# A linear-attention and mixture-of-experts kernel: four unread products at the start, and one PSUM bank in two halves for block 0's query work

## The chip, the cores and the metric

The kernel runs on one core of a Trainium2 chip. The metric is the device time of one execution, in microseconds (us). The core has a matrix engine (TensorE, PE in the profile; PEld is its weight load), VectorE (DVE), ScalarE (ACT), GpSimd (POOL) and SyncE (SP), which here only issues DMAs.

## The reference

Three parts follow each other; only the first matters for the change. Keys and queries are projected by the same weight, every row is shifted by its largest magnitude, and exp of plus and minus the result gives 256 features. The key features are summed against the values over each batch's 576 positions, and the query features are multiplied by that sum and divided by the denominator.

```
proj = einsum('bhsd,df->bhsf', x, w_phi)          # x is q or k; 64 -> 128
proj = proj - max(abs(proj), axis=-1)
phi  = concatenate([exp(proj), exp(-proj)], -1)
kv = einsum('bhsf,bhsd->bhfd', k_p, v);  z = sum(k_p, axis=2)
out = einsum('bhsf,bhfd->bhsd', q_p, kv) / (einsum('bhsf,bhf->bhs', q_p, z) + 1e-6)
```

There are 4 batches of 8 heads; the 2304 rows of all batches stand in a row. Behind it come an RMS norm with a gated layer (512 to 1536 to 512) and a soft mixture of 8 experts, both over all 2304 rows.

## The kernel before

The kernel has a first stage (keys, values, and the first block of queries), a long middle that runs over six blocks of 384 rows, and the experts' products at the end. All three are one program, whose order on each engine a scheduler lays out from dependencies and buffers.

**Tiles.** The first stage takes 18 tiles `ks[i]` of 128 rows. For each one `Front.project` (L503) makes two PSUM banks `P` with 8 products of 128 columns, four from weight rows 0 to 63 and four from rows 64 to 127, alternating. VectorE takes the largest magnitude (`mx`, L507) and the difference (`pr`, L511), ScalarE two exponentials (`kp`, L524 and L525). Then `kv_of` (L548) multiplies the features by the values `vt`: 4 products of 256 columns into `kacc0` and 4 into `kacc1`, with outputs that alternate between partitions 0 to 63 and 64 to 127. `z_of` (L557) makes 8 sums of 32 output partitions into `kacc2`. The loop projects tile i+2 while it multiplies tile i. After a batch's last row, `Evac` copies the three sums out, and `Evac.turn` (L585) transposes them through a bank `kvt`, which ScalarE or VectorE copies to `kv` (L594, L596).

**Block 0's queries.** `Rows`, a kind of `Turned`, handles the first 384 query rows. For each of four pairs of heads, c = 0 to 3, it makes three products `P` of 256 columns from `qraw` (`project`, L389; VectorE reads them as `qmx` and `qpr`), turns each with two transposes `T` (`turn`, L404; ScalarE reads them with two exponentials `e`, L406), and then multiplies with `kv` (`attend`, tile `o`, L449). `TURNED0` says into which half step of the key loop each one falls.

**PSUM.** There are eight banks. Three hold `kacc0` to `kacc2`; two have the tag `P` and hold the key projections; three have the tag `misc`, in turn for the first tile's two key projections, for `kvt`, for the queries' `P` and `T`, for `o` and for the last transposes `yT`. A buffer of `misc` can be written when the last reader of what it held has ended.

**The start.** `WARM = 3` products `idle` (L609) of a zeroed tile `still` run before anything has landed; nobody reads them. SyncE issues the loads of the first key tiles, values, constants and `qraw`. Between the tiles stands the conversion of nine weight pieces (`Conv`: `wraw`, 1 MB each, two ScalarE and three VectorE passes and a cast).

Of the kernel before, what the change touches and what calls it, by code (L numbers as in the profile page):

```python
# [7 lines left out]
F32 = mybir.dt.float32  # L8
# [8 lines left out]
NB, NH, SEQ, HD, DF = 4, 8, 576, 64, 128  # L17
# [3 lines left out]
TILES = NT // 128  # L21
# [7 lines left out]
KCONV, MCONV = (3, 2), (2, 2)  # L29
NX = 4  # L30
CFIRST = 7
WARM = 3
NLEFT = 2
ELEFT = 4
CTURN = 4
# [32 lines left out]
def tile_kernel(ctx: ExitStack, tc: tile.TileContext, q2T, qT, kT, v, wbd, wg, wv, wo, rmsg, phi, w1, w2, consts, out):  # L68
# [19 lines left out]
    def pool(stack, name, space=None, bufs=1, side="left"):  # L88
        kw = {} if space is None else {"space": space}
        if space is None:  # L90
            kw["side"] = side
        if space is not DRAM:
            kw["reuse_waits"] = "tile"
        return stack.enter_context(tc.tile_pool(name=name, bufs=bufs, **kw))
# [37 lines left out]
    class Conv:  # L132
# [3 lines left out]
        def __init__(self, sp, wp, key, bufs):  # L136
            self.sp, self.wp, self.key, self.bufs, self.n = sp, wp, key, bufs, 0
# [54 lines left out]
    kvt = {}  # L192
# [12 lines left out]
    class Q:  # L205
# [3 lines left out]
        def __init__(self, sp, ps, blk, bufs):  # L209
            self.sp, self.ps, self.blk, self.bufs = sp, ps, blk, bufs  # L210
            self.raw, self.x, self.e = {}, {}, {}

        def psum(self, name, shape):
            return self.ps.tile(shape, F32, tag="misc", name=name, bufs=self.bufs["misc"])

        def numerator(self, c, e):
            if c == 0:
                xraw[self.blk] = xp.tile([128, 4, BLK], F32, tag="xraw", name="xraw", bufs=1)
            num = self.psum("num", [128, BLK])
            for b, t0, t1 in block_parts(self.blk):  # L220
                for s in range(2):
                    for hh in range(2):
                        PE.matmul(out=num[64 * hh:64 * hh + 64, t0:t1], lhsT=kvt[b][:, 2 * c + hh, s, 0:HD],  # L223
                                  rhs=e[hh][:, s, t0:t1], start=s == 0, stop=s == 1, skip_group_check=True)
            return num
# [152 lines left out]
    class Turned(Q):  # L378
# [5 lines left out]
                SP.dma_start(out=self.raw[c], in_=q2T[self.blk, c])  # L384

        def project(self, c, i):
            p = self.psum("P", [128, 2, DF])
            o = p.rearrange("p h f -> p (h f)")
            PE.matmul(out=o, lhsT=self.raw[c][:, 128 * i:128 * i + 128], rhs=wbd_f, start=True, stop=True)  # L389
            mx = self.sp.tile([128, 2, 1], F32, tag="mx", name="qmx", bufs=2)  # L390
            self.pr = self.sp.tile([128, 2, DF], F32, tag="pr", name="qpr", bufs=self.bufs["pr"])
            DVE.tensor_reduce(out=mx, in_=p, axis=AX.X, op=ALU.max, apply_absolute_value=True)
            DVE.tensor_tensor(out=self.pr, in0=p, in1=mx.to_broadcast([128, 2, DF]), op=ALU.subtract)
            if i == TPB - 1:
                self.load(c + self.bufs["raw"])
            return self.pr

        def turn(self, c, i, pr):
            if i == 0:
                self.e2 = self.sp.tile([128, 2, 2, BLK], F32, tag="e", name="e2", bufs=self.bufs["e"])  # L400
                self.e[2 * c], self.e[2 * c + 1] = self.e2[:, 0], self.e2[:, 1]
            tp = self.psum("T", [128, 2, 128])
            for h in range(2):
                PE.transpose(out=tp[:, h], in_=pr[:, h], identity=ident)  # L404
            for s in range(2):
                ACT.activation(out=self.e2[:, :, s, 128 * i:128 * i + 128], in_=tp, func=AF.Exp, scale=1.0 - 2.0 * s)  # L406
# [72 lines left out]
    with ExitStack() as pk:  # L479
        kx = pool(pk, "kx")  # L480
        sp = pool(pk, "spk")
        psk = pool(pk, "psk", PSUM)
# [78 lines left out]
        class Evac:  # L561
# [17 lines left out]

            def turn(self, n):  # L580
                kv = self.kv
                tp = psk.tile([128, 2, 2, 128], F32, tag="misc", name="kvt", bufs=3)
                for c in range(2):
                    for s in range(2):
                        PE.transpose(out=tp[:, c, s], in_=self.sb[n][:, c, s], identity=ident)  # L585
                for c in range(2):
                    if n < 2:
                        o = kv[:, 4 * c + n:4 * c + n + 3:2, :, 0:HD].rearrange("p h s d -> p s h d")
                        i = tp[:, c].rearrange("p s (h d) -> p s h d", h=2)
                    else:  # L590
                        o = kv[:, c::2, :, HD].rearrange("p h s -> p s h")
                        i = tp[:, c].rearrange("p s (h r) -> p s h r", h=4)[:, :, :, 0]
                    if n == 1:
                        DVE.tensor_copy(o, i)  # L594
                    else:
                        ACT.copy(out=o, in_=i)  # L596
                if n == 2 and self.b >= 2:
                    SP.dma_start(out=kv_d[self.b], in_=kv.rearrange("p h s d -> p (h s d)"))

        kb = {"tag": "k", "raw": 4, "pr": 3, "P": ("P", 2)}  # L600
        ks = [K(sp, psk, kT, i, kb if i else dict(kb, P=("misc", 3))) for i in range(TILES)]
        ks[0].load(ACT)
        SP.dma_start(out=wbd_f, in_=wbd)
        still = sp.tile([128, 256], F32, tag="kvs0", name="still", bufs=1)
# [2 lines left out]
        idle = psk.tile([32, 256], F32, tag="acc0", name="idle", bufs=1)  # L607
        for _ in range(WARM):
            PE.matmul(out=idle, lhsT=still[:, 0:32], rhs=still, start=True, stop=True)  # L609
# [15 lines left out]
                k.shift(hf)  # L625
                k.exps(hf)
        fillers = []
        q0 = Rows(sp, psk, 0, {"misc": 3, "raw": 2, "pr": 3, "e": 2})
        qsteps = q0.steps(TURNED0[0:4], TURNED0[4:8], TURNED0[8:])
        qsteps = [[f for m, f in qsteps if m == n] for n in range(2 * TILES)]  # L630
        q0.begin()
# [87 lines left out]
    with ExitStack() as p2:  # L719
# [5 lines left out]
        sp = pool(tctx, "conv")  # L725
# [4 lines left out]
        def post(blk, x2):  # L730
# [177 lines left out]
            if blk == NBLK - 1:  # L908
                return finish
            return [turn(o) for o in range(TPB)] + [logits, rows, dturn, dispatch, combine, cturn]  # L910


# [19 lines left out]
        def gate(m, xs):  # L932
            g = wide("g", m, xs)
            t = mp.tile([128, BLK], F32, tag="t", name="t", bufs=2)
            ACT.activation(out=t, in_=g, func=AF.Tanh, scale=0.5)  # L935
            DVE.scalar_tensor_tensor(out=t, in0=t, scalar=1.0, in1=g, op0=ALU.add, op1=ALU.mult)  # L936
            return t
# [21 lines left out]
        t = gate(0, xs)  # L959
# [8 lines left out]
        for blk in range(NBLK):  # L968
            acc = [ps.tile([128, DM], F32, tag=f"acc{i}", name=f"acc{i}", bufs=1) for i in range(TPB)]
            qsteps, qnext = qnext or [], None  # L970
            if blk == 1:
                q1ctx.close()
                sp = pool(pctx, "post", side="right")
            if blk == NBLK - 1:
# [5 lines left out]
                sp = pool(pctx, "post", side="right")  # L980
# [32 lines left out]
            for m in range(MF):  # L1013
# [3 lines left out]
                if more:  # L1017
                    t = gate((m + 1) % MF, xs)
# [34 lines left out]
    with ExitStack() as p3:  # L1053
        sp = pool(p3, "sp3")
# [145 lines left out]
```

## Time and profile before

| what | us |
|---|---|
| runs of the kernel, lowest, median, highest | 705.16, 706.3, 707.02 |
| profiled execution | 705.7 |
| its span, first to last instruction | 703.9 |
| TensorE busy in the span | 689.4 (98%) |
| VectorE, ScalarE, GpSimd busy | 468.5, 329.1, 147.2 |
| first stage, to the first product of the middle | about 118 |

A busy share of 98% says that TensorE is rarely without an instruction. It does not say that each instruction goes as fast as it could: two products that use different rows or different output partitions of the array can run at once, and both count as busy. So the stage is read by the start times of its groups of products, and by the wait that each row shows in brackets.

### The profile page before, as it was taken

How to read it: one execution, taken by the hardware profiler on the slowest of the kernel's cores; microseconds unless marked ns; L12 is line 12 of the kernel's file. 1: busy time of each engine (PE TensorE's matmuls, PEld its weight loads, DVE VectorE, ACT ScalarE, POOL GpSimd, SP SyncE). 2: the span in 40 equal slices, each digit the busy share in tenths (PEclk: the TensorE clock that was granted, in tenths of full speed). 3: DMA queues.
4: the chain of work that ended last, by engine and by line, in shares of the span. 5: the costliest groups of instructions: out<-in, count | busy, mean ns of one | idle time of the engine just before them, and what ended most of it. 6: DMA issues, size and time to landing. Idle time of an engine off the chain costs nothing.

```text
span 703.9 us, 11807 instructions
## 1 busy us (share of the span) xinstructions
PE 689.4 (98%) x4653; PEld 571.3 (81%) x4653; DVE 468.5 (67%) x915; ACT 329.1 (47%) x687; POOL 147.2 (21%) x74
## 2 busy tenths in 40 slices
PE   7999999999999999999999999999999999999995
PEld 4667766988889898998989989899897999898443
DVE  4798995888875596765857669776585753423313
ACT  4878885687745443344432554425443232112103
POOL 0000000000003355133651326523364200000100
PEclk9999999999999999999999999999999999999997
DMA  6755535434211001010000100001000085577898
GB/s 224 280 170 192 195 107 181 143 120 160 79 40 33 3 24 40 0 57 12 24 9 1 57 13 23 9 0 57 1 1 8 1 305 234 190 284 256 323 367 291
DMA packets 25143, 79.42 MB, mean 113 GB/s; under 512 B 2688, under 2 KB 13376, under 8 KB 18688
## 3 DMA queue, kind: packets, MB, share of 16 engines
q1 hardware_dynamic: 24720, 77.52, 31.4%
q10 hardware_dynamic: 368, 1.15, 0.5%
q8 instruction: 36, 0.59, 0.3%
q14 instruction: 19, 0.16, 0.1%
HBM read 71.99 MB, written 6.67 MB: 112 GB/s over the span
## 4 chain that ended last, share of the span: by engine, by line
PE 96%; DMA 1%; ACT 1%; DVE 1%; issue 0%; SPq 0%; ACTq 0%
PE pg L928 22%; PE pv L928 22%; PE acc L953 7%; PE acc L954 7%; PE acc L955 7%; PE kacc L548 5%; PE num L223 4%; PE P L503 3%; PE kacc L557 3%; PE y L1088 2%; PE y L1072 2%; PE o L449 2%; PE P L389 1%; DMA wraw<-in_wo_dram 1%; PE x2tp L738 1%; PE qP L315 1%
## 5 line engine op out<-in xcount | busy, mean ns | idle before, releaser
L928 PE MATMUL pv<-xnh,wv 128*128 128x384 f32 x576 | 117.1, 343 | 0.0
L928 PE MATMUL pg<-xnh,wg 128*128 128x384 f32 x576 | 115.1, 342 | 0.3 <-ACT xnh L121 0.3
L318 POOL PARTITION_ALL_REDUCE qe<-qe x32 | 51.9, 1634 | 297.1 <-ACT qe L317 287.9
L928 PEld LDWEIGHTS pg<-xnh,wg 128*128 128x128 f32 x576 | 102.5, 188 | 5.8 <-ACT xnh L121 0.7
L928 PEld LDWEIGHTS pv<-xnh,wv 128*128 128x128 f32 x576 | 101.7, 188 | 1.5 <-issue 1.3
L349 POOL PARTITION_ALL_REDUCE qe<-qe x32 | 82.7, 2631 | 85.8 <-DVE qe L348 56.3
L121 ACT CAST hh<-t 128x384 fp32r<-128x384 f32 x72 | 36.7, 509 | 115.2 <-PE acc L954 77.6
L953 PE MATMUL acc<-wo,hh 128*128 128x512 f32 x216 | 87.2, 404 | 0.0
L954 PE MATMUL acc<-wo,hh 128*128 128x512 f32 x216 | 86.1, 399 | 0.0
L955 PE MATMUL acc<-wo,hl 128*128 128x512 f32 x216 | 85.3, 395 | 0.0
L124 DVE TENSOR_TENSOR hl<-t,hh 128x384 fp32r<-128x384 f32 x72 | 40.1, 557 | 63.3 <-ACT hh L121 63.2
L936 DVE SCALAR_TENSOR_TENSOR t<-t,pg 128x384 f32<-128x384 f32 x72 | 39.8, 553 | 57.9 <-ACT t L935 57.7
L935 ACT ACTIVATE t<-pg 128x384 f32<-128x384 f32 x72 | 35.1, 487 | 73.1 <-PE pg L928 72.7
L928 PE MATMUL pg<-xnl,wg 128*128 128x384 f32 x288 | 65.0, 342 | 0.0
L928 PE MATMUL pv<-xnl,wv 128*128 128x384 f32 x288 | 62.4, 339 | 0.0
L940 DVE TENSOR_TENSOR t<-t,pv 128x384 f32<-128x384 f32 x72 | 39.6, 549 | 24.6 <-PE pv L928 23.6
L928 PEld LDWEIGHTS pg<-xnl,wg 128*128 128x128 f32 x288 | 51.9, 188 | 1.6 <-DVE xnl L124 0.9
L928 PEld LDWEIGHTS pv<-xnl,wv 128*128 128x128 f32 x288 | 51.7, 188 | 0.0
L955 PEld LDWEIGHTS acc<-wo,hl 128*128 128x128 f32 x216 | 40.6, 188 | 10.2 <-DVE hl L124 0.3
L953 PEld LDWEIGHTS acc<-wo,hh 128*128 128x128 f32 x216 | 40.8, 189 | 7.3 <-issue 0.3
L954 PEld LDWEIGHTS acc<-wo,hh 128*128 128x128 f32 x216 | 40.6, 188 | 6.3
L548 PE MATMUL kacc<-kp,vt 128*64 128x256 f32 (+1 forms) x320 | 41.2, 393 | 2.3 <-ACT kp L525 2.3
(207 smaller groups left out, 1051.7 us busy)
## 6 DMA issues: line engine op xcount, KB each, us to landing
eu<-in_w_dram SPq DMA_DIRECT2D x32, 1024.0 KB, 6.6
wraw<-in_wg_dram SPq DMA_DIRECT2D x6, 1024.0 KB, 4.9
wraw<-in_wv_dram SPq DMA_DIRECT2D x6, 1024.0 KB, 5.6
wraw<-in_wo_dram SPq DMA_DIRECT2D x6, 1024.0 KB, 5.5
qraw<-in_qT_dram SPq DMA_DIRECT2D x32, 192.0 KB, 2.4
vt<-in_v_dram SPq DMA_DIRECT2D x18, 256.0 KB, 3.2
out_dram<-ob SPq DMA_DIRECT2D x18, 256.0 KB, 3.0
raw<-in_kT_dram SPq DMA_DIRECT2D x17, 256.0 KB, 2.9
```

The lines of the kernel that those rows point to most:

```text
L121: ACT.copy(out=hi, in_=src)
L124: (lo_eng or POOL).tensor_tensor(out=lo, in0=src, in1=hi.bitcast(F32), op=ALU.subtract)
L318: POOL.partition_all_reduce(e[:, 0], e[:, 1], channels=128, reduce_op=bass_isa.ReduceOp.absmax)
L349: POOL.partition_all_reduce(e[hh][:, 1], u, channels=128, reduce_op=bass_isa.ReduceOp.add)
L548: PE.matmul(out=kva[o0:o0 + 64, hh // 2], lhsT=self.vt[r0:r1, h], rhs=kp[r0:r1, hh].rearrange("p s f -> p (s f)"), start=first and hh < 2, ...
L928: PE.matmul(out=p, lhsT=w[:, a, c], rhs=x, start=n == 0, stop=n == 11)
L935: ACT.activation(out=t, in_=g, func=AF.Tanh, scale=0.5)
L936: DVE.scalar_tensor_tensor(out=t, in0=t, scalar=1.0, in1=g, op0=ALU.add, op1=ALU.mult)
L940: DVE.tensor_tensor(out=t, in0=t, in1=wide("v", m, xs), op=ALU.mult)
L953: PE.matmul(out=acc[i], lhsT=hh[:, s], rhs=w[:, 0], start=m == 0, stop=False)
L954: PE.matmul(out=acc[i], lhsT=hh[:, s], rhs=w[:, 1], start=False, stop=False)
L955: PE.matmul(out=acc[i], lhsT=hl[:, s], rhs=w[:, 0], start=False, stop=m == MF - 1)
```

## The change

`WARM` goes from 3 to 4. The tag `misc` goes from three banks to two. The freed bank becomes the tag `halves`, one tile of [128, 2, 2, 128] floats, which fills the bank; `half` hands out its two halves in turn. Block 0's query products `P` and their transposes `T`, which took a `misc` bank each, take a half instead. `q1` and the later blocks have no `half` in their `bufs` and stay as they were.

```
-WARM = 3
+WARM = 4
...
+        def half(self, name):
+            if "half" not in self.bufs:
+                return self.psum(name, [128, 2, 128])
+            if not self.halves:
+                t = self.ps.tile([128, 2, 2, 128], F32, tag="halves", name="halves", bufs=1)
+                self.halves = [t[:, 0], t[:, 1]]
+            self.halves.reverse()
+            return self.halves[0]
...
         def project(self, c, i):
-            p = self.psum("P", [128, 2, DF])
+            p = self.half("P")
...
-            tp = self.psum("T", [128, 2, 128])
+            tp = self.half("T")
...
-                tp = psk.tile([128, 2, 2, 128], F32, tag="misc", name="kvt", bufs=3)
+                tp = psk.tile([128, 2, 2, 128], F32, tag="misc", name="kvt", bufs=2)
...
-        ks = [K(sp, psk, kT, i, kb if i else dict(kb, P=("misc", 3))) for i in range(TILES)]
+        ks = [K(sp, psk, kT, i, kb if i else dict(kb, P=("misc", 2))) for i in range(TILES)]
...
-        q0 = Rows(sp, psk, 0, {"misc": 3, "raw": 2, "pr": 3, "e": 2})
+        q0 = Rows(sp, psk, 0, {"misc": 2, "half": True, "raw": 2, "pr": 3, "e": 2})
```

The scheduler lays out the first stage anew. Behind it TensorE's order is the same but for a dozen products of the first gate, where one of `pv` moves ahead of those of `pg`; VectorE's and ScalarE's orders also differ in the first of the middle's six blocks. TensorE's order is shown at two places. In the lines of the changed kernel L514 is the key projection (L503 before), L559 and L568 are `kv_of` and `z_of` (L548, L557), L400 and L415 are the query product and its transposes (L389, L404), and L620 is `idle`.

First, TensorE at the start of the program, before the change, from the unread products to the first two query products:

```order
L609 MATMUL idle<-still 32x256 x3
L503 MATMUL P<-wbd_f,raw 128x128 x16
L548 MATMUL kacc_190<-kp,vt 64x256 x4
L557 MATMUL kacc_192<-kp,small 32x256
L548 MATMUL kacc_191<-kp,vt 64x256
L503 MATMUL P<-wbd_f,raw 128x128 x8
L548 MATMUL kacc_191<-kp,vt 64x256 x3
L557 MATMUL kacc_192<-kp,small 32x256 x7
L548 MATMUL kacc_190<-kp,vt 64x256 x4
L503 MATMUL P<-wbd_f,raw 128x128 x8
L548 MATMUL kacc_191<-kp,vt 64x256 x4
L557 MATMUL kacc_192<-kp,small 32x256 x8
```

Two query products come behind these rows; now one of them stands ahead of the first `kacc` product, as the same place reads after the change:

```order
L620 MATMUL idle<-still 32x256 x4
L514 MATMUL P<-wbd_f,raw 128x128 x16
L400 MATMUL halves<-wbd_f,qraw 128x256
L559 MATMUL kacc_191<-kp,vt 64x256 x4
L559 MATMUL kacc_192<-kp,vt 64x256
L514 MATMUL P<-wbd_f,raw 128x128 x8
L559 MATMUL kacc_192<-kp,vt 64x256 x3
L568 MATMUL kacc_193<-kp,small 32x256 x8
L559 MATMUL kacc_191<-kp,vt 64x256 x3
L514 MATMUL P<-wbd_f,raw 128x128 x8
L559 MATMUL kacc_191<-kp,vt 64x256
L559 MATMUL kacc_192<-kp,vt 64x256 x4
```

The first query product moved up past 16 `kacc` and 16 sum products, and the single sum (x1, x7) is gone. Second, TensorE between the sums of tile 2 and those of tile 3, before the change, with the semaphores that each waits for (DMAHW is a DMA's):

```order
L404 MATMUL T<-cst,qpr 128x128 [waits DVE_49]
L404 MATMUL T<-cst,qpr 128x128
L389 MATMUL P<-wbd_f,qraw 128x256 [waits PE_49]
L404 MATMUL T<-cst,qpr 128x128 [waits DVE_49,PE_49]
L404 MATMUL T<-cst,qpr 128x128
L503 MATMUL P<-wbd_f,raw 128x128 [waits DMAHW6_49,DVE_49,PE_49]
L503 MATMUL P<-wbd_f,raw 128x128 [waits DVE_49,PE_49]
L503 MATMUL P<-wbd_f,raw 128x128 x6
L548 MATMUL kacc_190<-kp,vt 64x256 [waits DMAHW2_49,Activation_49]
L548 MATMUL kacc_190<-kp,vt 64x256 x3
L548 MATMUL kacc_191<-kp,vt 64x256 [waits Activation_49]
L548 MATMUL kacc_191<-kp,vt 64x256 x3
```

The query work of that step stood together there, ahead of the unbroken groups of 8 projections and 8 `kacc` products. After the change the same place reads:

```order
L415 MATMUL halves<-cst,qpr 128x128 [waits DVE_49]
L415 MATMUL halves<-cst,qpr 128x128
L514 MATMUL P<-wbd_f,raw 128x128 [waits DMAHW6_49,DVE_49,PE_49]
L514 MATMUL P<-wbd_f,raw 128x128 [waits DVE_49,PE_49]
L514 MATMUL P<-wbd_f,raw 128x128 x3
L400 MATMUL halves<-wbd_f,qraw 128x256 [waits Activation_49]
L514 MATMUL P<-wbd_f,raw 128x128 x3
L559 MATMUL kacc_191<-kp,vt 64x256 [waits DMAHW2_49]
L559 MATMUL kacc_191<-kp,vt 64x256 x3
L559 MATMUL kacc_192<-kp,vt 64x256
L415 MATMUL halves<-cst,qpr 128x128 [waits DVE_49]
L559 MATMUL kacc_192<-kp,vt 64x256 x3
```

The third query product now stands inside the group of 8 projections (5 and 3), and the second pair of transposes inside the group of 8 `kacc` products (5 and 3). Over the whole first stage the 160 `kacc` products stand in 23 runs before and 31 after, and the 144 projections in 17 and 23. Taken two by two within a run, the `kacc` products make 81 pairs or singles before, and 90 after. No number of products differs but that of `idle`.

## Rows read from the trace of the kernel before

**Rows 1.** The page: busy time of each engine, and the chain that ended last.
```profile
PE 689.4 (98%) x4653; PEld 571.3 (81%) x4653; DVE 468.5 (67%) x915; ACT 329.1 (47%) x687; POOL 147.2 (21%) x74
PE 96%; DMA 1%; ACT 1%; DVE 1%; issue 0%; SPq 0%; ACTq 0%
```
**Rows 2.** Windows: span, busy us per engine (instructions), clock (1.00 full), DMA share, GB/s.
```profile
0.00:118.00 118.00, 112.66 (x1140) 73.34 (x1140) 94.89 (x166) 87.06 (x162) 0.20 (x4) 0.99 0.55 188
118.00:300.00 182.00, 181.81 (x1058) 161.29 (x1059) 137.69 (x255) 100.95 (x204) 35.92 (x17) 1.00 0.21 71
300.00:640.00 340.00, 340.00 (x1914) 305.32 (x1913) 215.60 (x443) 128.84 (x292) 108.34 (x51) 1.00 0.20 70
```
**Rows 3.** TensorE's two longest waits in the first 118 us: total us, times, longest.
```profile
PE kacc L548 <- ACT kp L525: 2.3, 1, 2.3
PE P L389 <- ACT kv L596: 1.3, 1, 1.3
```
**Rows 4.** TensorE's timeline to 22 us: start, duration, records (two a product), wait before.
```profile
1.18 2.77 PE L609 MATMUL idle<-still 128*32 128x256 f32 x6 [1.18 <-DVE small L606]
4.25 2.97 PE L503 MATMUL P<-wbd_f,raw 64*128 64x128 f32 x32 [0.30 <-DMA raw<-in_kT_dram]
9.48 1.88 PE L548 MATMUL kacc<-kp,vt 128*64 128x256 f32 x8 [2.26 <-ACT kp L525]
11.30 1.06 PE L557 MATMUL kacc<-kp,small 128*32 128x256 f32 x2
12.29 1.00 PE L548 MATMUL kacc<-kp,vt 128*64 128x256 f32 x2
13.21 1.17 PE L503 MATMUL P<-wbd_f,raw 64*128 64x128 f32 x16
14.31 1.08 PE L548 MATMUL kacc<-kp,vt 128*64 128x256 f32 x6
15.32 1.06 PE L557 MATMUL kacc<-kp,small 128*32 128x256 f32 x14
16.32 1.08 PE L548 MATMUL kacc<-kp,vt 128*64 128x256 f32 x8
17.33 1.49 PE L503 MATMUL P<-wbd_f,raw 64*128 64x128 f32 x16
...
20.76 1.13 PE L389 MATMUL P<-wbd_f,qraw 128*128 128x256 f32 x4
21.82 1.16 PE L503 MATMUL P<-wbd_f,raw 64*128 64x128 f32 x16
```
**Rows 5.** Windows of 1 us, columns as in Rows 2: the granted clock falls and rises.
```profile
9.00:10.00 1.00, 0.52 (x4) 0.34 (x6) 1.00 (x3) 1.00 (x3) 0.00 (x0) 0.81 1.05 399
13.00:14.00 1.00, 1.00 (x15) 0.79 (x15) 0.00 (x0) 0.00 (x0) 0.00 (x0) 0.98 0.03 12
```
**Rows 6.** DMA issued between 5.0 and 5.3 us: KB each, us to landing.
```profile
qraw<-in_q2T_dram SPq DMA_DIRECT2D x1, 192.0 KB, 5.4
```
**Rows 7.** TensorE's timeline, a plain tile (8 kacc, 8 sums) and query work behind it.
```profile
42.56 1.95 PE L548 MATMUL kacc<-kp,vt 128*64 128x256 f32 x16
44.44 1.07 PE L557 MATMUL kacc<-kp,small 128*32 128x256 f32 x16
45.44 0.66 PE L585 MATMUL kvt<-cst,kvs 128*128 128x128 f32 x4
45.94 0.38 PE L404 MATMUL T<-cst,qpr 128*128 128x128 f32 x2
```
**Rows 8.** Timeline of all engines from 36 to 42 us: the wait at 40.84.
```profile
36.99 1.19 ACT L146 ACTIVATE wt<-wraw 128x1024 f32<-128x1024 f32 x1 [0.74 <-DMA wraw<-in_wo_dram]
40.84 0.70 PE L389 MATMUL P<-wbd_f,qraw 128*128 128x256 f32 x2 [1.33 <-ACT kv L596]
41.07 0.41 DVE L393 TENSOR_TENSOR qpr<-P,qmx 128x256 f32<-128x256 f32 x1
```
**Rows 9.** Timeline of ScalarE: the two exponentials of the transposes at 45.94.
```profile
46.35 0.66 ACT L406 ACTIVATE e<-T 128x256 f32<-128x256 f32 x2
```

More of the change, by code (lines that the diff above doesn't have):

```diff
@@ L211, in __init__ @@
             self.raw, self.x, self.e = {}, {}, {}
+            self.halves = None
         def psum(self, name, shape):
             return self.ps.tile(shape, F32, tag="misc", name=name, bufs=self.bufs["misc"])
+        def half(self, name):
[6 more added lines that the diff above has]
+            return self.halves[0]
         def numerator(self, c, e):
```

## The prediction

> **What bounds the kernel now.** I read the page's busy times and its chain first: TensorE is busy for 98% of the span and carries 96% of the chain [rows 1]. The windows by stage then say where anything is left. From 118 to 640 us TensorE is busy in 521.81 of 522 us, and the first 118 us, where the change lies, have 5.3 us without an instruction [rows 2]. Of these, 1.2 us lie ahead of the first instruction, and the longest two waits are 2.3 and 1.3 us [rows 3]. The other engines have slack: VectorE 95 and ScalarE 87 of 118 us [rows 2]. So a microsecond that TensorE gains or loses in the first stage reaches the end undiminished, unless it runs into one of those waits.
>
> The third view is TensorE's timeline, and it must be read by the starts of groups, since busy time hides how well two products share the array. A plain tile's 8 `kacc` products (16 records) take 44.44 - 42.56 = 1.88 us, its 8 sums 1.00 us [rows 7], its 8 projections 1.09 to 1.10 us (13.21 to 14.31) [rows 4]. Now the broken group at the start: after one `kacc` product stood alone, the other three took 14.31 to 15.32 = 1.01 us. Four took 16.32 to 17.33, also 1.01 us [rows 4]. Three cost as much as four: a product without a partner costs what a pair costs. That is the row on which this prediction rests. The same for the sums: 7 took 1.00 us like 8, and the one that was cut off cost 12.29 - 11.30 = 0.99 us more at the low clock [rows 4].
>
> **The start.** Before: three unread products to about 4.25, the projections of two tiles, a wait to 9.48 for ScalarE's features, then `kacc` at half clock until the granted clock rises at 13.0 [rows 4, 5]. After: one more unread product of two records, 2.77 / 6 = 0.46 us or a little less, delays the first projection by some 0.35 us, as the tile landed at 4.25 [rows 4]. This cost is covered, by a wait that the new order creates: a query product now stands ahead of the first `kacc`. Its `qraw` is issued between 5.0 and 5.3 us and takes 5.4 us to land [rows 6], so it can't run before about 10.5 (10.4 to 10.7), while `kacc` ran at 9.48 and would be ready at about 9.7. Behind it on TensorE are queued the `kacc` products and then tile 2's projections, and VectorE and ScalarE wait for those.
>
> From 10.5: the query product costs 1.13 / 2 = 0.56 us at the full clock [rows 4], at half clock twice that less overlap, 0.95; four `kacc` products 1.82 at half clock (9.48 to 11.30), of which the last 0.2 us fall behind 13.0; one alone 0.5; so tile 2's projections start at about 13.65 instead of 13.21. But the lone sum of 0.99 us is gone and one query product is already done. Adding the groups of the new order from there, 1.10 + 1.01 + 1.00 + 1.01 + 1.10 + 1.45 (five `kacc`: three pairs' time) + 1.00 + 0.53, tile 4's projections start at 21.85 against 21.82 [rows 4]: +0.0 us. This holds if the clock rises at 13.0 again. It was low from about 9.8, since TensorE had idled from 7.2 to 9.48 [rows 4, 5]; now it idles to 10.5. If the rise comes as much later as the work does, 1.0 us at half clock costs 0.5; at most I count another stretch like that of 9.8 to 13.0, 1.6 us; and below, 0. I take **+0.5** (0 to 1.6).
>
> **The broken groups.** From tile 4's projections on, the new order breaks the 8 `kacc` products of a tile at eight more places (81 pairs or singles become 90; the ninth is in the start, counted above). Each leaves two products without a partner where there was a pair. By the lone product's share, 1.01 us for three less half of 1.01 for two, a break costs 0.50 us [rows 4]; from below 1.88 / 4 = 0.47 for the pair's time alone [rows 7], from above 0.58 with a new start of a run: 1.45 + 1.01 - 1.88. I take 0.50: **+4.0 us** (3.7 to 4.6). The 8 projections are broken five times, as 5 and 3, 4 and 4, or in three. Here the rows are less plain: eight cost 1.10 us at 13.21 and 1.41 at 17.33 [rows 4], where the order of rows also leaves some without a partner. Nothing to 0.4 us each; I take 0.2: **+1.0 us** (0 to 2.0). The moved query products and transposes cost what they cost before; two more runs of them, 0.1 each: **+0.2**.
>
> **The wait at 40.84.** The second query product of head pair 1 waited 1.33 us for ScalarE's copy of `kvt`, since three `misc` banks were in use [rows 8]. With a bank of its own it doesn't: **-1.33 us**. What is late next: the same product now stands behind a projection group and one `kacc` product, and waits for VectorE to have read the first one, which ended at 41.07 + 0.41 = 41.5, because VectorE stood behind ScalarE's work on a weight piece that landed at 36.99 [rows 8]. TensorE gets there at about 42.6 with the delays above, and that piece's load is issued in turn behind loads that wait for TensorE, so it moves along: **+0.35** (0 to 1.0).
>
> **New waits at the shared bank.** No row of before shows one tile used by halves. The order shows that the third query product waits for ScalarE, though the half that it writes was last read by VectorE: so the halves are guarded as one bank, and a half can't be filled while the other is being read. The price: transposes at 45.94, the exponentials from 46.35 to 47.01 [rows 7, 9], so 1.07 us from the first to the bank's release if ScalarE is free. In the new order five projections or four stand in between, 0.28 + 0.8 or 0.28 + 0.6 us. This leaves nothing to 0.2 us, and ScalarE's key exponentials ahead of them may add one of 0.5 us. Four such places, two of them with 0.25: **+0.5** (0 to 2.5). Where the transposes wait for VectorE, 1.5 to 3.5 us of TensorE's work lie between; I cost these at nothing, covered by those products.
>
> The Trainium skill, "PSUM — Partial Sum Buffer", section "PSUM bank collisions raise a hardware error", says the same against this change: two engines must not touch one bank and quadrant at once even in different columns, so software guards by bank. By it the two halves are one buffer and the 0.5 us stand; were the halves free of each other, the sum would be 0.5 us lower. No run here shows the collision itself.
>
> The changed orders of VectorE and ScalarE in the middle's first block I cost at nothing: TensorE waited 0.19 us in 118 to 300 [rows 2]; up to 1 us if that cover is gone.
>
> **The sum.** +0.5 + 4.0 + 1.0 + 0.2 - 1.33 + 0.35 + 0.5 = **+5.2 us**. Against the profiled execution of 705.7 us (span 703.9) this is 710.9; that execution lies 0.6 us below the median of the three runs, 706.3, so in medians I expect **711.5 us**. The bounds of the terms together give +2.4 (0 + 3.7 + 0 + 0 - 1.33 + 0 + 0) to +11.6; with not all at one end, +3 to +8, 709.3 to 714.3.
>
> **The rivals.** *The same time as before.* If a product that has lost its partner overlaps with the transpose or projection put beside it, the breaks cost only a new start each, 0.07 us (1.01 for four less half of 1.88), 0.6 in all; the projections nothing. Then +0.5 + 0.6 + 0.2 - 1.33 + 0.35 + 0.5 = +0.8, 707.1 us. Against it: the three products at 14.31 had the first sums right behind them and overlapped with nothing [rows 4]. For it: that row is one single case. It turns from slower to not slower when a break costs under about 0.2 us. Chance 0.16.
>
> *Faster, by the clock.* If `qraw` landed before 8 us, the early query product would fill the idle stretch, the clock would not fall at 9.8, and 1.6 us would be saved [rows 5]; with the 1.33 us and cheap breaks this gives 706.3 + 0.8 - 0.5 - 1.6 - 0.35 - 0.5 = 704.2, and decides only where both hold, as the breaks' 4 us otherwise outweigh it. The 5.4 us to land speak against it [rows 6]. Chance 0.06.
>
> *The shared bank rules.* If each of the twelve head-pair steps makes TensorE wait 0.4 us for the bank, one exponential's time, that is 4.8 instead of 0.5, and with the clock's late rise (1.6) the sum is 5.2 + 4.3 + 1.1 = +10.6, 716.9 us. For it: VectorE and ScalarE are in order, with weight pieces of over 1 us in their queues. Against it: their slack of 23 and 31 us [rows 2]. Chance 0.13. The forecast has the remaining 0.65.
>
> **How the numbers follow.** A measurement tells about 0.3%, 2.1 us, from no change: 704.2 to 708.4. The forecast is slower throughout, as is the last rival: 0.78; the first rival and a small part of the second are within: 0.17; faster 0.05. The range leaves out most of the faster rival and half of the last: 706.8 to 715.5 us.
>
> **What would show it.** In the profile after: the query product at about 10.5 with a wait on its load ahead of it; `kacc` groups of 5 and 3 that take 1.4 and 1.0 us; no 1.33 us wait at 41 but one of some tenths; a first product of the middle at about 123 instead of 118; the middle's length unchanged. I am wrong if five and three together take under 2.1 us, or if TensorE's idle time in the stage is over 8 us.

## The result

The changed kernel takes **714.88 us** (median of 4 runs, 713.05 to 715.22) against 706.3 us before. The ratio is 1.0123, with a 95% interval of 1.0109 to 1.0137: slower by 8.6 us. The profiled execution has a span of 713.4 us, where that of before had 703.9.

The page of the changed kernel, with the same two lines as [rows 1], shows TensorE still at 98%, with 9.3 us more busy time for only two more records:

```profile
PE 698.7 (98%) x4655; PEld 574.4 (81%) x4655; DVE 469.3 (66%) x915; ACT 329.3 (46%) x687; POOL 147.1 (21%) x74
PE 91%; DVE 3%; DMA 2%; ACT 2%; issue 1%; SPq 0%; ACTq 0%
```

Windows by stage, columns as in [rows 2] (the first stage now ends at 127.54 us instead of 118.05):

```profile
0.00:127.50 127.50, 122.41 (x1142) 76.62 (x1142) 95.85 (x166) 87.40 (x162) 0.20 (x4) 0.99 0.51 174
127.50:300.00 172.50, 172.03 (x1010) 152.66 (x1011) 129.39 (x231) 97.63 (x198) 35.42 (x17) 1.00 0.22 75
300.00:640.00 340.00, 340.00 (x1914) 305.28 (x1913) 221.33 (x462) 130.94 (x295) 108.69 (x52) 1.00 0.18 63
```

The whole difference lies in the first stage: 127.54 - 118.05 = 9.49 us, and 713.4 - 703.9 = 9.5 us. Behind it TensorE is as full as before. TensorE's waits up to 130 us (total us, times, longest), which answer to [rows 3]; 1.2 us ahead of `idle` and 0.3 us ahead of the middle's first product stand in both kernels and are left out:

```profile
PE halves L400 <- DMA qraw<-in_q2T_dram: 2.3, 1, 2.3
PE halves L400 <- DVE qpr L404: 0.8, 1, 0.8
PE kvt L596 <- ACT kvx L607: 0.3, 1, 0.3
PE halves L400 <- ACT e L417: 0.2, 1, 0.2
```

So TensorE does not wait longer. It is slower while it works. Its timeline (start, duration, records, wait before) shows the start, up to tile 4's projections at 21.90, which stood at 21.82 before [rows 4]:

```profile
9.93 1.22 PE L400 MATMUL halves<-wbd_f,qraw 128*128 128x256 f32 x2 [2.31 <-DMA qraw<-in_q2T_dram]
11.08 2.61 PE L559 MATMUL kacc<-kp,vt 128*64 128x256 f32 x10
13.62 1.17 PE L514 MATMUL P<-wbd_f,raw 64*128 64x128 f32 x16
...
21.90 1.17 PE L514 MATMUL P<-wbd_f,raw 64*128 64x128 f32 x16
```

And the next tile, where a group of eight projections and a group of eight `kacc` products are broken as 5 and 3, to be read against the plain tile of [rows 7]:

```profile
25.88 0.44 PE L415 MATMUL halves<-cst,qpr 128*128 128x128 f32 x2
26.24 0.93 PE L514 MATMUL P<-wbd_f,raw 64*128 64x128 f32 x10
27.34 0.70 PE L400 MATMUL halves<-wbd_f,qraw 128*128 128x256 f32 x2 [0.17 <-ACT e L417]
27.97 0.71 PE L514 MATMUL P<-wbd_f,raw 64*128 64x128 f32 x6
28.61 1.51 PE L559 MATMUL kacc<-kp,vt 128*64 128x256 f32 x10
30.05 0.44 PE L415 MATMUL halves<-cst,qpr 128*128 128x128 f32 x2
30.42 1.08 PE L559 MATMUL kacc<-kp,vt 128*64 128x256 f32 x6
31.42 1.07 PE L568 MATMUL kacc<-kp,small 128*32 128x256 f32 x16
```

By starts, less the wait in brackets, the five `kacc` products take 30.05 - 28.61 = 1.44 us and the three 31.42 - 30.42 = 1.00: 2.44 instead of 1.88. The projections take 0.93 and 0.64: 1.57 instead of 1.10. The query product between them takes 0.63.

In the trials below the kernel before has medians of 704.16 to 706.0 us. Its own executions differ by 2 to 3 us, with the mean granted clock (spans of 701.2 to 702.1 us at 0.997, 703.2 to 705.0 at 0.991 to 0.993), so each ratio is to the runs of before beside it. Where two profiles are compared, I start at tile 4's projections, behind the clock's low stretch.

### The profile page after: what moved, and what is told of

It is laid out like the page before. It is cut to its first block, busy times and chain, and to the rows that moved or that the text cites. A ratio compares the mean times of both kernels' runs of the same rounds, so it can differ in the third digit from the quotient of the medians.

```text
span 713.4 us, 11804 instructions
## 1 busy us (share of the span) xinstructions
PE 698.7 (98%) x4655; PEld 574.4 (81%) x4655; DVE 469.3 (66%) x915; ACT 329.3 (46%) x687; POOL 147.1 (21%) x74
## 3 DMA queue, kind: packets, MB, share of 16 engines
q10 hardware_dynamic: 368, 1.15, 0.5%
## 4 chain that ended last, share of the span: by engine, by line
PE 91%; DVE 3%; DMA 2%; ACT 2%; issue 1%; SPq 0%; ACTq 0%
PE pg L939 21%; PE pv L939 21%; PE acc L964 7%; PE acc L965 7%; PE acc L966 7%; PE kacc L559 4%; PE num L234 4%; PE y L1099 2%; PE y L1083 2%; PE P L514 2%; PE kacc L568 2%; PE o L460 2%; DMA wraw<-in_wo_dram 1%; PE halves L400 1%; PE x2tp L749 1%; PE qP L326 1%
## 5 line engine op out<-in xcount | busy, mean ns | idle before, releaser
L559 PE MATMUL kacc<-kp,vt 128*64 128x256 f32 (+1 forms) x320 | 46.6, 395 | 0.0
```

The lines of the kernel that those rows point to most:

```text
L559: PE.matmul(out=kva[o0:o0 + 64, hh // 2], lhsT=self.vt[r0:r1, h], rhs=kp[r0:r1, hh].rearrange("p s f -> p (s f)"), start=first and hh < 2, ...
```

## The experiments

**Which of the two does it, the start or the order?** The first two runs keep one half of the change each.

```
-WARM = 3
+WARM = 4
```

> The kernel before with WARM = 4 alone; the three misc banks stay. TensorE's order becomes that of the changed kernel up to tile 4's projections (a query product ahead of the first kacc product) and stays that of before behind it: P in 17 runs, kacc in 22 runs of 82 pairs or singles, where before has 81 and the changed kernel 90. Theory (broken groups): the start is free, since the changed kernel's tile 4 began its projections at 21.90 us against 21.82 before; +0.1 to +0.6, so 706.4 to 706.9 us. Rival (the start costs, through the clock or the wait for qraw): +2 us or more, over 708.3, tile 4's projections at 23.5 or later.

Measured: 705.94 us, ratio 1.0016 [1.0001, 1.003]. The product order changes up to tile 4 only, and the time by 0.16%, about 1.1 us. The changed kernel with the warm-up undone is the other half:

```
-WARM = 4
+WARM = 3
```

> The changed kernel with WARM = 3 again: two misc banks and the bank in halves stay. TensorE starts as before the change, and its groups are broken as in the changed kernel (kacc in 32 runs of 89 pairs or singles, P in 24 runs). Theory (broken groups): all of the loss stays, 714 to 715.5 us, and the pitch of kacc and P stays within 0.5 us of the changed kernel's 44.5 and 23.0. Rival (the start costs): most of the loss goes, 706 to 710 us.

Measured: 712.44 us, ratio 1.0113 [1.0084, 1.0143]. The loss goes with the bank. The start is not its main place.

**Is it the bank's guard or the broken order?** The next run gives the changed kernel the order of before, as far as the shared bank allows: from the third step on, TensorE takes the products as the code issues them.

```
-        for i in range(TILES):
+        def step(i):
...
+        for i in range(TILES):
+            if i < 2:
+                step(i)
+            else:
+                placed(lambda: step(i), PE.engine)
```

> The changed kernel with four unread products and the bank in halves, but TensorE's order from tile 4's projections on is held to the order in which the code issues it: the same runs as in the kernel before with WARM = 4 (P in 17 runs, kacc in 22 runs of 82). Against that kernel only the banks differ; against the changed kernel only the order. Theory A (the broken groups are the price by which the scheduler avoids waits for the shared bank): kacc, P, query products and transposes fall back to the pitch of before, -9 us, and waits come in their place. At each of four places where two transposes, a query product and two transposes follow each other, the product waits for the two exponentials (25.88 to 27.29 less 0.44, about 0.9 us) and the second transposes for VectorE's two passes (27.34 to 29.53 less 0.6, about 1.6 us), so 2.5 us each, and two more places of 1 to 1.6 us: 12 us, less the 1.33 us wait that is gone. 714 to 719 us, with 9 to 13 us of waits at the lines L400 and L415. Rival B (the halves can be used apart, the broken groups are a needless choice of the scheduler): hardly a wait, 704.5 to 707 us.

Measured: 727.9 us, ratio 1.0327 [1.0302, 1.0352], slower than even theory A's 719. TensorE's waits in its trace, and the first place of four:

```profile
PE halves L415 <- DVE qpr L404: 5.1, 4, 2.0
PE halves L400 <- ACT e L417: 4.7, 4, 1.6
PE halves L400 <- DVE qpr L404: 4.0, 2, 2.4
```

```profile
25.84 0.44 PE L415 MATMUL halves<-cst,qpr 128*128 128x128 f32 x2
27.31 0.70 PE L400 MATMUL halves<-wbd_f,qraw 128*128 128x256 f32 x2 [1.03 <-ACT e L417]
28.98 0.44 PE L415 MATMUL halves<-cst,qpr 128*128 128x128 f32 x2 [0.98 <-DVE qpr L404]
```

The waits come to 13.8 us, near the 12 that theory A asked for. Most of the rest is the clock. A window of this run's trace, and the same window of the run with four unread products, whose order of products this one has (span, busy us, clock third from the end):

```profile
24.00:60.00 36.00, 29.81 (x282) 17.27 (x279) 26.35 (x39) 24.33 (x46) 0.00 (x0) 0.91 0.51 167
```

```profile
24.00:60.00 36.00, 34.60 (x371) 23.43 (x363) 30.96 (x48) 29.24 (x53) 0.00 (x0) 1.00 0.63 232
```

TensorE is idle for 6.2 of the 36 us here, and the granted clock's mean falls to 0.91. From 60 to 100 us it is 0.91 again, with 5.7 us idle. So the unbroken order is no way out with this bank: whole groups, in that order, wait. That the scheduler breaks them for this reason fits, but no run shows it.

Two orders and two sets of banks make four kernels, and the fourth corner of that square is the changed order on the banks of before. A table holds TensorE's order of the first stage, product by product, as the changed kernel has it, and links each to the one ahead of it; three `misc` banks, no halves.

```
+ORDER = [(0, 20), (68, 69), (28, 33), (20, 21), (22, 23), (21, 22), (23, 28), (33, 44), (52, 55), (44, 45), (46, 47), (45, 46), (47, 52), (55, 68),
...
+        mine = [i for i in nc.cur_bb.bb.instructions[traced0:] if i.engine == PE.engine]
+        mine = [mine[n] for a, b in ORDER for n in range(a, b) if n < len(mine)]
+        for x, y in zip(mine, mine[1:]):
+            tc.add_manual_dep(y, x.name, nosync, reason="placed")
```

> The banks of before (three misc, no halves) with four unread products, and TensorE's order in the first stage held to that of the changed kernel, product by product: kacc in 31 runs, P in 23. It is the fourth corner of a square: the order of before with the banks of before was +0.2%, the changed order with the shared bank +1.1 to +1.2%, the order of before with the shared bank +3.3%. Theory A (the broken groups alone are the loss; the bank only made the scheduler break them): as slow as the changed kernel, +7 to +9 us on before (ratio 1.010 to 1.013), kacc's pitch over 43 us, waits for VectorE and ScalarE under 0.5 us. Rival (the loss is in the guard of the shared bank, in waits or in slower products on that bank): +0 to +2 us (1.000 to 1.003).

Measured: 713.11 us, ratio 1.0124 [1.0109, 1.0139]: the changed kernel's ratio, without its bank. The same place as above, with the same durations and no wait:

```profile
25.93 0.70 PE L394 MATMUL P<-wbd_f,qraw 128*128 128x256 f32 x2
26.55 0.71 PE L508 MATMUL P<-wbd_f,raw 64*128 64x128 f32 x6
27.19 1.51 PE L553 MATMUL kacc<-kp,vt 128*64 128x256 f32 x10
28.63 0.44 PE L409 MATMUL T<-cst,qpr 128*128 128x128 f32 x2
29.00 1.08 PE L553 MATMUL kacc<-kp,vt 128*64 128x256 f32 x6
30.01 1.07 PE L562 MATMUL kacc<-kp,small 128*32 128x256 f32 x16
```

This settles the place: the loss is the order. Against the run with four unread products, whose banks are the same, the groups from tile 4 on take, summed over starts and less waits: `kacc` 38.46 us instead of 33.77, projections 17.91 instead of 15.33, query products 6.55 instead of 5.52, transposes 4.14 instead of 3.54.

**Why does a broken group cost that?** My row was the lone product of [rows 4]. I tested the partner directly: the same runs, with neighbours of the same output half.

```
-                for hh in range(4):
+                for hh in (0, 2, 1, 3):
```

> The kernel before with the four products of a kacc bank issued in the order of heads 0, 2, 1, 3, so that neighbours write the same 64 output partitions twice in a row; nothing else moves (kacc in 23 runs as before, but 102 pairs or singles instead of 81). Theory (a product without a partner costs a pair's time, 0.43 to 0.50 us): +21 x 0.43 to 0.50 = +9 to +10.5 us, 715.3 to 716.8 us, and kacc's pitch 39.6 + 9 to 10.5. Rival (partners don't matter, a run costs only its start): 706.3 us.

Measured: 706.24 us, ratio 1.0011 [0.9997, 1.0025]. A plain tile in its timeline:

```profile
40.23 2.00 PE L548 MATMUL kacc<-kp,vt 128*64 128x256 f32 x16
42.16 1.07 PE L557 MATMUL kacc<-kp,small 128*32 128x256 f32 x16
```

The eight products take 42.16 - 40.23 = 1.93 us instead of 1.88. The theory as I had put it here, pairs of neighbours, is false. Before dropping the partner altogether I put it farther away: four products of the lower half, then four of the upper.

```
-                for f in (self.kv_of, self.z_of):
+                for o in range(2):
                     for hf in range(2):
-                        f(hf, part)
+                        self.kv_of(hf, part, o)
+                for hf in range(2):
+                    self.z_of(hf, part)
...
-                for hh in range(4):
+                for hh in (o, o + 2):
```

> The kernel before with the eight kacc products of a tile issued as four into output partitions 0 to 63 and then four into 64 to 127, instead of in turn; the runs, 23 of them, stay. Exchanging neighbours alone cost 0.05 us a tile. Theory A (a product runs beside another one if it stands one or two places from it, and not farther): four and four can overlap only in the middle; a tile's 1.88 us becomes 2.3 (five steps of 0.43 and 0.15) to 3.2 us (seven steps), so on some 17 tiles +7 to +22 us, 712 to 727 us. Rival (each half has a queue deep enough for a whole tile, and distance does not matter): 1.9 us a tile, no change, 704 to 707 us; then a lone partner is not why an odd group costs what the next even one does.

Measured: 720.71 us (2 runs), ratio 1.0217 [1.0183, 1.0252]. A plain tile in its timeline:

```profile
43.50 2.86 PE L550 MATMUL kacc<-kp,vt 128*64 128x256 f32 x16
46.29 1.07 PE L559 MATMUL kacc<-kp,small 128*32 128x256 f32 x16
```

The eight take 46.29 - 43.50 = 2.79 us instead of 1.88. The single records of that tile (two a product) tell why: the first four start one at a time, 0.22 to 0.27 us apart, the next eight in twos at most 0.06 us apart, the last four one at a time. I read this as two products alone, two pairs of the third with the fifth and the fourth with the sixth, and two products alone. So the halves do run side by side, and a product finds a partner beside it or two places on, but not three or four. In this run the products also change between `kacc0` and `kacc1` after every two; no record starts later at such a change. Nothing in a run says how the array keeps the order. The Trainium skill, "TensorE: Matmul & The Clock Gate", Part 3 (packing small matmuls), has matrix products start and end strictly in the order of the program. By that alone the exchange of neighbours would have cost at least one more step of 0.43 us a tile; it cost 0.05, so here the measurement decides against its strict form, while four and four agree with its direction.

The third test leaves the interruptions in the changed kernel and moves each query product and each pair of query transposes one product later where it stood behind an odd number (5 and 3 become 6 and 2):

```
+ORDER = [(0, 20), (68, 69), (28, 33), (20, 21), (22, 23), (21, 22), (23, 28), (33, 44), (52, 55), (44, 45), (46, 47), (45, 46), (47, 52), (55, 68),
...
```

> The changed kernel, banks and all, with its order edited from tile 2's sums on: a query product or a pair of transposes that stands behind an odd number of a tile's eight kacc products or projections is moved one product later, so that 5 and 3 become 6 and 2, 7 and 1 become 8, 1 and 7 become 2 and 6. The number of interruptions hardly falls (kacc 29 runs instead of 31, P 23). Theory A (a broken group costs the lost partner: 0.47 us of kacc, 0.27 us of P, and only some 0.1 us for the change of work): kacc 7 x 0.47 = 3.3 and P 5 x 0.27 = 1.3 us come back, so 4 to 5 us less than the changed kernel, +3.5 to +5 us on before (ratio 1.005 to 1.007). Theory B (each interruption costs the same 0.5 us, wherever it stands, since the groups drain the array; the reordering of pairs, which cost nothing, speaks for this): within 1.5 us of the changed kernel, 1.010 to 1.013.

Measured: 711.46 us, ratio 1.0093 [1.0075, 1.0111], between the two. The profiles are plainer than the times: span 709.8 instead of 713.4 us. `kacc` from tile 4 on takes 35.36 us instead of 38.54, so 3.2 us came back, as theory A had it (3.3). The rows:

```profile
26.46 0.94 PE L519 MATMUL P<-wbd_f,raw 64*128 64x128 f32 x12
27.55 0.70 PE L405 MATMUL halves<-wbd_f,qraw 128*128 128x256 f32 x2 [0.16 <-ACT e L422]
28.18 0.49 PE L519 MATMUL P<-wbd_f,raw 64*128 64x128 f32 x4
28.60 1.52 PE L564 MATMUL kacc<-kp,vt 128*64 128x256 f32 x12
30.05 0.44 PE L420 MATMUL halves<-cst,qpr 128*128 128x128 f32 x2
30.42 0.65 PE L564 MATMUL kacc<-kp,vt 128*64 128x256 f32 x4
31.00 1.07 PE L573 MATMUL kacc<-kp,small 128*32 128x256 f32 x16
```

Six products take 1.45 us, what five took, and two take 0.58. The projections gave nothing back (18.14 us instead of 17.93): their 6 and 2 take 0.93 and 0.42, a little under 5 and 3, but one half group of four took 1.25 us instead of 0.86: its eight records start one at a time, and why they did I don't know.

With the runs of all lengths in this trace and in that of the fourth corner, the steps of `kacc` are complete (us from the start of a run to the next start, at the full clock):

| products in the run | 1 | 2 | 3 | 4 | 5 | 6 | 7 | 8 |
|---|---|---|---|---|---|---|---|---|
| `kacc` | 0.58 | 0.58 | 1.01 | 1.01 | 1.44 | 1.45 | 1.87 | 1.88 |

That is 0.43 us for each two, rounded up, and 0.15 for each run. For projections in alternating order it is 0.42 for 2, 0.64 for 3, 0.87 for 5, and 1.10 for 8: 0.22 for each two, and 0.2 for each run. An odd break of a `kacc` group costs 0.58 us, an even one 0.15; a break of a projection group 0.2 to 0.4, and 0.62 (twice 0.86 less 1.10) where it falls 4 and 4 with three of one half in the first four.

**Can the bank be used without the loss?** Here what stood inside a tile's eight projections or eight `kacc` products is moved behind that group:

```
+ORDER = [(0, 20), (68, 69), (28, 33), (20, 21), (22, 23), (21, 22), (23, 28), (33, 44), (52, 55), (44, 45), (46, 47), (45, 46), (47, 52), (55, 68),
+(69, 71), (72, 73), (71, 72), (73, 96), (99, 107), (96, 97), (107, 115), (97, 99), (115, 174), (175, 191), (174, 175), (191, 205), (208, 216), (205,
...
```

> The changed kernel, banks and all, with its order edited from tile 2's sums on: whatever stands inside a tile's eight projections or eight kacc products is moved behind that group, so that each use of the shared bank has a whole group between it and the next (P 17 runs, kacc 22). Theory A (broken groups are the loss, and a group of 1.1 to 1.9 us hides the guard of the shared bank, 0.9 us of ScalarE or 1.6 us of VectorE): all the 5 us of kacc and 2 to 3 us of P come back, waits at the halves under 2.5 us, and the wait of 1.33 us of before is gone: -1 to +2 us on before (0.998 to 1.003). Rival (the guard's waits come whenever the groups stay whole, as they did in the order of before): over 4 us of waits at the halves, +5 us or more (1.007).

Measured: 708.89 us, ratio 1.0061 [1.0043, 1.0079]; better by half, and above theory A's range. `kacc` is back at 33.77 us, exactly its value on the unbroken order, and the longest wait at the bank is this one:

```profile
26.17 0.70 PE L405 MATMUL halves<-wbd_f,qraw 128*128 128x256 f32 x2 [0.87 <-ACT e L422]
```

What stays are the query products and transposes that stand alone: 6.54 and 4.23 us instead of 5.52 and 3.54 in the run with four unread products, and two projection groups whose products the scheduler issued as three and three, 1.41 us each instead of 1.10.

The halves themselves were taken out too, with one plain buffer in their place:

```
-            if not self.halves:
-                t = self.ps.tile([128, 2, 2, 128], F32, tag="halves", name="halves", bufs=1)
-                self.halves = [t[:, 0], t[:, 1]]
-            self.halves.reverse()
-            return self.halves[0]
+            return self.ps.tile([128, 2, 128], F32, tag="halves", name=name, bufs=1)
```

> The changed kernel with a plain bank of one buffer in the place of the two halves: each query product and each pair of transposes takes a new tile of [128, 2, 128] from a tag with one buffer. TensorE's order comes out the same, product by product. Theory (the halves are guarded as one bank, so they are one buffer): the same time as the changed kernel within 1.5 us, +1.0 to +1.3% on before, the same waits of 1.0 us in all. Rival (the halves let a write start beside a read of the other half): more waits, 2 us or more slower than the changed kernel.

Measured: 714.61 us, ratio 1.0131 [1.0108, 1.0154]: the changed kernel's time. The order is the same, product by product. The two halves are worth one buffer: with unbroken groups, too, the query product at 27.31 us waited 1.03 us for ScalarE, which read the other half. The Trainium skill, "PSUM — Partial Sum Buffer", section "PSUM bank collisions raise a hardware error", has software guard PSUM by bank and quadrant (32 partitions), not by address. By that the two halves are one buffer, and these measurements agree.

**What the bank was to bring, without it.** In the kernel before, with its own banks, the one product that waited 1.33 us [rows 8] goes behind the eight projections that followed it.

```
+ORDER = [(0, 19), (27, 31), (35, 36), (31, 32), (19, 20), (21, 22), (20, 21), (22, 27), (32, 35), (36, 43), (51, 55), (43, 44), (45, 46), (47, 48),
+(44, 45), (46, 47), (48, 51), (55, 173), (174, 182), (173, 174), (182, 208), (209, 210), (208, 209), (210, 313), (314, 315), (313, 314), (315, 612)]
```

> The kernel before, three misc banks and three unread products, with its own order held, but for one product: the query product that waited 1.33 us for ScalarE's copy of kvt at 40.84 us stands behind the eight projections that followed it (1.1 us). Theory: the wait falls to 0.2 us or less and nothing else moves, -1.0 to -1.3 us (ratio 0.998); this is all that the shared bank was to bring, without it. Rival (the stage is bound elsewhere, or the copies come later as the wait moves): no change within 0.3 us.

Measured: 703.48 us (12 runs), ratio 0.9986 [0.9974, 0.9998]. From tile 4's projections to the middle it takes 95.20 us instead of 96.23. The product now starts behind the projections without a wait:

```profile
36.86 1.16 PE L505 MATMUL P<-wbd_f,raw 64*128 64x128 f32 x16
38.10 0.70 PE L391 MATMUL P<-wbd_f,qraw 128*128 128x256 f32 x2
38.73 1.95 PE L550 MATMUL kacc<-kp,vt 128*64 128x256 f32 x16
```

The last run applies the steps of `kacc` and of the sums to the start as well; only the head of the table differs:

```
+ORDER = [(0, 19), (27, 31), (35, 39), (19, 20), (21, 22), (20, 21), (22, 27), (31, 35), (39, 43), (51, 55), (43, 44), (45, 46), (47, 48), (44, 45),
...
```

> The kernel before with the query product of 40.84 us moved behind the eight projections, as in the last run that was 0.14% faster, and with the first tile's products regrouped: four kacc, four sums, tile 2's projections, four kacc, four sums, instead of 4, 1, 1, projections, 3, 7. By the measured steps (a kacc run of n products takes 0.43 us for each two, rounded up, and 0.15; sums 0.25 for each four) the start loses a lone kacc product (0.58 + 1.01 become 1.01) and a split sum (two groups of about 1.0 become two of 0.5), 1.0 to 1.5 us at the full clock and up to 2.5 at half. Theory: 1 to 2 us below that run, 0.3 to 0.45% below before. Rival (the start is bound by ScalarE's exponentials and tile 2's projections, a saved product becomes a wait): the same as that run, -0.1 to -0.2%.

Measured: 702.99 us (12 runs), ratio **0.9963** [0.9949, 0.9977], faster than both kernels. Its start, to be read against [rows 4]:

```profile
11.27 1.08 PE L559 MATMUL kacc<-kp,small 128*32 128x256 f32 x8
12.28 1.41 PE L505 MATMUL P<-wbd_f,raw 64*128 64x128 f32 x16
13.62 1.08 PE L550 MATMUL kacc<-kp,vt 128*64 128x256 f32 x8
14.63 0.64 PE L559 MATMUL kacc<-kp,small 128*32 128x256 f32 x8
15.20 1.08 PE L550 MATMUL kacc<-kp,vt 128*64 128x256 f32 x8
...
20.71 1.16 PE L505 MATMUL P<-wbd_f,raw 64*128 64x128 f32 x16
```

Tile 4's projections start at 20.71 instead of 21.82, 1.1 us earlier, with the same mean granted clock from 9 to 14 us (0.66), and the first stage ends at 115.76 instead of 118.05.

## Why the prediction was right, and where its sum was off

The direction, the place and the main mechanism hold: slower by the order of TensorE's first stage, and 714.88 us lies within 706.8 to 715.5. The likeliest time, 711.5, was 3.4 us too low. The measured time lies even above the 709.3 to 714.3 that I gave to the sum, and inside the range only because that was drawn wider, to take in half of the last rival; so far the hit is luck.

Of the signs that I named, five and three `kacc` products took 1.44 and 1.00 us, the wait of 1.33 us went, and from the middle's first product on the span kept its length (585.9 us in both profiles). The query product came at 9.93 instead of 10.5, and the middle's first product at 127.54, not at about 123.

Step by step, against the two profiles (from tile 4's projections on, starts less waits):

| step | forecast | profile |
|---|---|---|
| start, to tile 4's projections | +0.5 | +0.1 |
| broken `kacc` groups | +4.0 | +4.7 |
| broken projection groups | +1.0 | +2.6 |
| query products and transposes as runs of their own | +0.2 | +1.6 |
| the wait at 40.84, and what is late next | -1.33 + 0.35 | -1.33 + 0.80 |
| waits at the shared bank | +0.5 | +0.2 |
| a wait of `kvt` for ScalarE at the end of the stage | 0 | +0.3 |
| `kvt`, `o`, `yT` and sums | 0 | +0.5 |
| sum | +5.2 | +9.5 |

- **The start** is right but for the load: the query product ran at 9.93, not 10.5. The clock rose a little later (0.83 in the window of 13 to 14 us, 0.98 in [rows 5]); tile 2's projections started at 13.62, where I had 13.65. Two errors cancel there: the load landed 0.6 us earlier, and the query product and the five `kacc` products took 1.15 and 2.54 us by starts, where I had 0.95 and some 2.2. That TensorE's idle time alone makes the clock fall is not borne out (last section). And the 0.1 us holds where the clock fell in both kernels; where it stayed at 1.00, tile 4's projections started at 19.24 and 19.48 us with the old start (the runs with one moved product and with exchanged neighbours) and at 19.79, 20.68 and 20.72 with the new one (whole groups, four unread products, the fourth corner), 0.3 to 1.5 us later.
- **The `kacc` term** had the right row and the right size, 0.58 us for an odd break instead of 0.50. I had 0.58 as the upper bound, "with a new start of a run": the 0.15 us of each run that I left out of the value. The reason that I gave, that a product needs a partner, holds with a correction: exchanging neighbours costs next to nothing (0.05 us), four and four 0.9 us a tile.
- **The projections** are the first mis-sized term. I saw that the rows were less plain, priced a break at 0.2 us and counted five. There were six, at 0.43 on the mean, somewhat above my bound of 0.4.
- **Query products and transposes** are the second: "what they cost before". By starts, a query product takes 0.43 to 0.44 us ahead of transposes and 0.63 ahead of projections or `kacc`; a pair of transposes 0.21 to 0.28 ahead of a query product or `kvt`, and 0.31 to 0.38 elsewhere. In before they stood together, and I did not ask what they would cost apart. These two terms make 3.0 of the 4.3 us.
- **The waits** came as forecast in their sum: TensorE waited 0.8 us for VectorE at 43.62, where I had 0.35, and 0.2 for ScalarE, where I had 0.5; 1.0 in place of 0.85. The 1.33 us went.
- **The rival of the same time** fell with five and three at 2.44 us. **Faster by the clock** fell with the load at 9.93. **The shared bank rules** fell as a cost of the changed order, but the run with unbroken groups shows it is real: 13.8 us of waits stood ready, and with the broken order they did not come. I had priced the waits that were left and not asked why the scheduler had broken the groups.

## What to carry to other kernels

Where products of half the array run two at a time, count a group's time by its runs: steps of one pair, rounded up, and a start for each run. A buffer taken away or shared can cost nothing in waits and still cost much, when a scheduler fills the waits by breaking such groups; so compare the order first, and price every place where a run begins. The wait that a new buffer is to remove can be filled, as here, by moving one instruction behind the group that follows it.

## What the runs showed of the chip beyond that

The clock at the start is not settled by the wait ahead of it. In the kernel before, `kacc` started at 9.48 us after a wait of 2.26 us, with the clock at 0.50, the lower of its two levels (1.2 instead of 2.4 GHz), from 10 to 13 us [rows 4, 5]; one window of that stretch:

```profile
10.00:11.00 1.00, 1.00 (x8) 0.35 (x4) 1.00 (x3) 0.80 (x2) 0.00 (x0) 0.50 1.05 402
```

In the run with one moved product it started at 8.50 after the same wait, and the clock stayed at 1.00 (timeline, then a window of 1 us):

```profile
8.50 1.08 PE L550 MATMUL kacc<-kp,vt 128*64 128x256 f32 x8 [2.26 <-ACT kp L527]
```

```profile
9.00:10.00 1.00, 1.00 (x8) 0.26 (x4) 1.00 (x3) 0.80 (x2) 0.00 (x0) 1.00 0.93 349
```

Four `kacc` products took 1.01 us there and 1.82 at the low clock. What decides it the runs don't show. And waits can cost more than their sum: in the run with unbroken groups TensorE was idle in the first stage for 19.1 us, 12.9 more than in the same order on separate banks, but the span is 22.9 us longer (725.8 against 702.9). From tile 4's projections on, `kacc` and the projections took 5.5 us more in stretches of low clock (its mean is 0.51 from 52 to 59 us, behind waits of 1.59 and 0.98 us, and 0.91 in the two stretches above), query products and transposes, which the waits set apart, 2.8 us more; the start took 1.2.
